# Chunk 1's rows let go by the first q, k weight piece, and a new order of all engines

## The chip, the cores and the metric

The kernel runs on one core of a Trainium2 chip. The core has engines with instruction queues of their own: PE (matmul, with its weight load shown as PEld), DVE (vector), ACT (scalar), POOL (GpSimd) and SP, which here only issues DMAs; 16 DMA engines move the data. The metric is the device time of one execution in microseconds (us). Of the kernel before there are three runs: 194.37, 195.01 and 195.72 us, median 195.01.

## What is computed

A pre-norm transformer layer on 2048 rows of 512 channels in bf16: attention with 32 heads of 16 channels over a dilated window of 8 keys, then a gated feed-forward of width 1376. Cut to what matters:

```python
def _A_ref(x, wqkv, wo):
    H = 32; Dh = D // H; W, dil = 8, 2
    q, k, v = (x @ wqkv).reshape(B, S, 3, H, Dh)          # split in three, heads first
    idx = arange(S)[:, None] - arange(W)[None, :] * dil    # keys at s, s-2, ... s-14
    kg, vg = k[idx], v[idx]                                # masked where idx < 0
    attn = softmax(einsum("bhsd,bhswd->bhsw", q, kg) * Dh ** -0.5)
    return einsum("bhsw,bhswd->bhsd", attn, vg) @ wo

def _B_ref(x, W_gate, W_up, W_down):
    gate, up = x @ W_gate, x @ W_up
    return ((gate * (gate > 0)) * up) @ W_down

h  = x + _A_ref(layernorm(x), A_wqkv, A_wo)
h2 = h + _B_ref(layernorm(h), B_W_gate, B_W_up, B_W_down)
```

## The kernel before

The rows are worked in four chunks of 512 (`tk` = 0 to 3), each of four row blocks of 128. A chunk goes through these stages; the names in quotes are the plan's own keys for its steps.

- First layer norm: statistics and their aggregation on DVE ("xst", line 467; "xag", line 470), the root on ACT ("xrl", "xre"), for chunks 1 and 3 a bias on DVE ("xnb", line 488), the normalization on DVE for chunks 0 and 2 ("xxn", line 502) and on ACT for chunks 1 and 3 (line 499), then the transposition, on PE ("xtp", line 531) with an eviction by ACT ("xte") or, for chunk 0's row block 1, by DVE ("xtv", line 545). Chunk 3's transposition is done by DMA.
- q, k and v: twelve groups of matmuls (line 572), eight for q and k and four for v, each evicted by ACT (line 580). In chunk 0 the first six q, k groups are cut in three pieces ("qka", "qkb", "qkc"), so that the first two row blocks and the first two weight pieces can be used early. A matmul with 512 columns is a whole group's quarter; the pieces have 256.
- Scores: products of q with shifted keys on DVE ("pr"; in chunk 0 half steps at line 637, elsewhere line 620), summed over channels on PE ("sc1" for the far four keys and "sc0" for the near four, line 628, each over all its products), the exponential on ACT, for chunk 0 a mask on DVE ("mk").
- The spread of the weights by DMA from SP (line 756), products with shifted values on DVE ("mu"), their sum, of which the first step is an accumulating DMA from POOL ("ta", line 831), the division (line 795 in chunk 0), and the output projection on PE ("wo", line 867).
- Second layer norm, gate and up matmuls (line 940), their evictions and product, the down projection (line 990) and the output.

PE takes work of several chunks in turn: while DVE is busy with chunk 0's attention, PE does the q, k and v groups of chunks 1 to 3.

**What sets the order.** The program is written as a plan of 751 steps, each with an engine, a duration, its dependencies and the buffers that it takes. `RANK` holds one number for each step, in the order in which the plan adds them. An engine's steps are issued strictly in the order of their numbers; the planner's own times, which come from its table of durations and due times, only decide which buffer of a pool each step gets. `XT` and `WT` (lines 377 and 378) are those due times of the first loads: the four row blocks of chunk 0, the four of chunk 1, chunks 2 and 3; and of the weights.

**The first loads.** They are issued by hand, ahead of the plan, in lines 316 to 347. SP and ACT each issue two of chunk 0's row blocks and two of the four pieces of the q, k weight, in turn: block 0 and piece 0 on SP, block 1 and piece 1 on ACT, block 2 and piece 2 on SP, block 3 and piece 3 on ACT. Everything behind these goes out on SP, held back by gates: POOL copies a few bytes into the place that a later load will fill, from a place that an earlier load fills. The later load must wait for that copy, and the copy for the earlier load.

```python
nc.gpsimd.tensor_copy(out=x_sm[0:1, BPC:2 * BPC, 0:1], in_=x_sm[0:1, 3, 0:BPC])      # line 334
for j in range(BPC, 2 * BPC):
    nc.sync.dma_start(x_sm[:, j:j + 1, :], x_rows[:, j:j + 1, :])                    # line 336
nc.gpsimd.tensor_copy(out=wv_sb[0:1, 0, 0:1], in_=wqk_sb[0:1, 3, 0:1])               # line 337
nc.sync.dma_start(wv_sb[:], w3_r[:, :, 2 * D:3 * D])
nc.gpsimd.tensor_copy(out=x_sm[0:1, 2 * BPC, 0:1], in_=x_sm[0:1, 2 * BPC - 1, 0:1])  # line 339
```

So chunk 1's four row blocks wait for chunk 0's block 3, the v weight for piece 3 of the q, k weight, and the rows of chunks 2 and 3 (and, on SP behind them, the output projection's weight and the gate weight) for chunk 1's last row block. Before chunk 0's first q, k matmul PE runs matmuls on a blank tile (lines 421 and 429).

Of the kernel before, what the change touches and what calls it, by code (L numbers as in the profile page):

```python
# [16 lines left out]

RANK = [
# [38 lines left out]
]  # L57


# [143 lines left out]
def kernel(  # L203
# [11 lines left out]
    nc = tc.nc  # L215
# [24 lines left out]
    BPC = CS // P  # L240
# [25 lines left out]
    x_sm = sb.tile([P, NTB, D], BF16, name="x_sm")  # L266
    wqk_sb = sb.tile([P, NT, 2 * D], BF16, name="wqk_sb")
# [45 lines left out]
    def setup():  # L313

        w3_r = A_wqkv.rearrange("(dt p) f -> p dt f", p=P)
        for i in range(2):
            for n, q in enumerate((nc.sync, nc.scalar)):
                j = 2 * i + n
                q.dma_start(x_sm[:, j:j + 1, :], x_rows[:, j:j + 1, :])
                q.dma_start(wqk_sb[:, j:j + 1, :], w3_r[:, j:j + 1, 0:2 * D])  # L320
        nc.scalar.preload_act_table_set("natural_log_exp_and_others")
        V.memset(warm[:], 0.0)
        make_identity(nc, identity[:])
        nc.gpsimd.memset(eps_t[:], EPS)
        nc.gpsimd.iota(ci[:], pattern=[[0, 1]], base=0, channel_multiplier=1)
        nc.gpsimd.iota(sel_i[:], pattern=[[1, H]], base=0, channel_multiplier=0)
        nc.gpsimd.iota(sp_i[:], pattern=[[1, H], [0, DQ]], base=0, channel_multiplier=0)
        nc.gpsimd.iota(sm_i, pattern=[[0, 4], [1, H]], base=0, channel_multiplier=0)
        nc.gpsimd.iota(mk_i[:], pattern=[[1, PADL]], base=0, channel_multiplier=0)
        nc.gpsimd.memset(kT[:, :, 0:PADL], 0.0)  # L330
        nc.gpsimd.memset(vT[:, :, 0:PADL], 0.0)


        nc.gpsimd.tensor_copy(out=x_sm[0:1, BPC:2 * BPC, 0:1], in_=x_sm[0:1, 3, 0:BPC])
        for j in range(BPC, 2 * BPC):
            nc.sync.dma_start(x_sm[:, j:j + 1, :], x_rows[:, j:j + 1, :])  # L336
        nc.gpsimd.tensor_copy(out=wv_sb[0:1, 0, 0:1], in_=wqk_sb[0:1, 3, 0:1])
        nc.sync.dma_start(wv_sb[:], w3_r[:, :, 2 * D:3 * D])
        nc.gpsimd.tensor_copy(out=x_sm[0:1, 2 * BPC, 0:1], in_=x_sm[0:1, 2 * BPC - 1, 0:1])
        for tk in range(2, NCK):  # L340
            nc.sync.dma_start(x_sm[:, tk * BPC:(tk + 1) * BPC, :], x_rows[:, tk * BPC:(tk + 1) * BPC, :])

        nc.sync.dma_start(wo_sb[:], A_wo.rearrange("(p t) f -> p t f", t=NT))
        for n in "gud":
            for i in range(2):
                if n not in LATE:
                    f_load(n, i)


        for n, (op, by) in enumerate(((ALU.arith_shift_right, 2), (ALU.bitwise_and, H - 1),  # L350
                                      (ALU.arith_shift_right, 5))):
            V.tensor_scalar(out=tmp[:, n:n + 1], in0=ci[:], scalar1=by, scalar2=None, op0=op)
        V.tensor_copy(out=cf[:, 0:3], in_=tmp[:])
        V.tensor_scalar(out=cf[:, 2:3], in0=cf[:, 2:3], scalar1=1.0 * DIL, scalar2=None, op0=ALU.mult)
        V.tensor_scalar(out=cf[:, 3:4], in0=cf[:, 2:3], scalar1=4.0 * DIL, scalar2=None, op0=ALU.add)
        V.tensor_scalar(out=sel[:], in0=sel_i[:], scalar1=cf[:, 0:1], scalar2=None, op0=ALU.is_equal)
        V.tensor_scalar(out=spread[:], in0=sp_i[:], scalar1=cf[:, 1:2], scalar2=None, op0=ALU.is_equal)
        V.tensor_scalar(out=same[:], in0=sm_i, scalar1=cf[:, 1:2], scalar2=None, op0=ALU.is_equal)
        for hf in range(2):
            V.tensor_scalar(out=mask[:, hf, :], in0=mk_i[:], scalar1=cf[:, 2 + hf:3 + hf],  # L360
                            scalar2=None, op0=ALU.is_ge)
# [12 lines left out]
    TDD, TDL = 1.3, 1.5  # L374
    NWARM, NFILL = 56, (13, 10, 0)
    NHALF = 6
    XT = (3.47, 3.64, 5.45, 5.97, 8.4, 8.7, 9.25, 9.75, 15.9, 17.65)
    WT = (7.65, 7.65, 5.0, 13.7, 19.0, 24.95, 22.4, 28.8)
    DMAT = (('h',2,0),('h',2,2),('h',3,0),('h',3,2),('h',1,0),('x',3,0),('x',3,2))

    EARLY = (1, 2, 3)
# [695 lines left out]
```

## Time and profile before

| | |
|---|---|
| median of three runs | 195.01 us (194.37 to 195.72) |
| the profiled execution | 196.09 us |
| its span, first to last instruction | 194.2 us |
| granted PE clock | 1.000 |
| DMA moved | 24.61 MB, mean 127 GB/s |
| HBM read, written | 8.42 MB, 2.10 MB |

The profile is of one execution. Times in it are microseconds from the span's start. "Busy" is the time an engine spent in instructions; matmuls are pipelined and their ends are modelled, so for PE the distance from start to start says more than a duration. A row names the source line, the engine, the operation, and the tile written and read. "Idle before, releaser" is how long an engine waited ahead of an instruction and what ended that wait. The chain of waits is followed back from the last instruction, at each step to what released it.

### The profile page before, as it was taken

The numbers are of one execution on the slowest core, as the hardware profiler recorded it, in microseconds if no ns is written. First come the engines' busy times: TensorE is split into PE (matmuls) and PEld (weight loads), VectorE is DVE, ScalarE is ACT, GpSimd is POOL, SyncE is SP. The second block draws the span as 40 slices with busy tenths as digits, with TensorE's granted clock in tenths as the row PEclk, the third lists the DMA queues.
The fourth block names the chain that finished last, engine by engine and source line by source line (L and its number), as shares of the span: only waits on it lengthen the run. The fifth ranks groups of instructions, "written<-read, shape, count | busy, mean of one in ns | idle before, by whom it ended". The sixth has DMA issues, their size and how long they took to land.

```text
span 194.2 us, 3099 instructions
## 1 busy us (share of the span) xinstructions
PE 188.5 (97%) x1141; PEld 98.3 (51%) x1141; DVE 150.7 (78%) x243; ACT 115.7 (60%) x241; POOL 17.0 (9%) x35
## 2 busy tenths in 40 slices
PE   7897999999999999999999999999999999999994
PEld 7884455555445344644454444445454444554443
DVE  6769999999999999979999988699966424021432
ACT  3568989964799682974362679612875911267500
POOL 3000001420000004200046000001100000000000
PEclk9999999999999999999999999999999999999999
DMA  5759776999900807996169935733400141203021
GB/s 194 205 164 358 262 168 127 181 192 246 378 29 16 199 4 147 190 181 161 27 122 187 202 64 153 173 81 57 108 0 0 34 101 57 81 0 108 0 64 47
DMA packets 25214, 24.61 MB, mean 127 GB/s; under 512 B 11408, under 2 KB 21488, under 8 KB 25200
## 3 DMA queue, kind: packets, MB, share of 16 engines
q1 hardware_dynamic: 22176, 16.26, 30.1%
q0 software_dynamic: 2304, 7.34, 20.6%
q10 hardware_dynamic: 720, 0.82, 1.3%
q8 instruction: 9, 0.15, 0.3%
q14 instruction: 5, 0.04, 0.1%
HBM read 8.42 MB, written 2.10 MB: 54 GB/s over the span
## 4 chain that ended last, share of the span: by engine, by line
PE 89%; DMA 5%; ACT 2%; issue 1%; DVE 1%; SPq 1%; ACTq 0%; POOL 0%
PE bank L940 36%; PE bank L990 20%; PE bank L572 17%; PE bank L867 7%; DMA x_sm<-in_A_x_dram 5%; PE bank L628 4%; PE bank L907 3%; PE bank L531 2%; ACT row L499 1%; DVE st L467 1%; SPq L336 1%; ACT quad L580 0%; PE bank L713 0%; PE bank L870 0%; ACT kT L580 0%
## 5 line engine op out<-in xcount | busy, mean ns | idle before, releaser
L940 PE MATMUL bank<-quad,wgu_sb 128*128 128x512 bf16 x320 | 72.4, 379 | 0.0
L940 PEld LDWEIGHTS <-wgu_sb 128*128 128x128 bf16 x320 | 31.0, 98 | 36.7 <-issue 1.3
L990 PE MATMUL bank<-wd_sb,gT 128*128 128x512 bf16 (+3 forms) x198 | 39.1, 355 | 0.0
L947 ACT ACTIVATE gr<-bank 128x512 bf16<-128x512 f32 x40 | 23.8, 607 | 22.6 <-PE bank L940 21.0
L572 PE MATMUL bank<-quad,wqk_sb 128*128 128x512 bf16 (+1 forms) x152 | 29.3, 345 | 0.3 <-ACT rs L480 0.3
L990 PEld LDWEIGHTS <-gT 128*128 128x128 bf16 (+1 forms) x198 | 18.5, 98 | 19.7
L944 ACT CAST up_sb<-bank 128x512 bf16<-128x512 f32 x40 | 22.7, 597 | 8.7 <-PE bank L940 5.3
L788 DVE TENSOR_TENSOR big<-big,vT 128x4096 bf16<-128x4096 bf16 x12 | 27.0, 2285 | 0.7 <-DVE big L620 0.5
L620 DVE TENSOR_TENSOR big<-quad,kT 128x4096 bf16<-128x4096 bf16 x12 | 27.1, 2286 | 0.0
L968 DVE TENSOR_TENSOR gT<-gr,up_sb 128x1024 bf16<-128x1024 bf16 x20 | 13.7, 689 | 16.4 <-ACT up_sb L944 13.4
L572 PEld LDWEIGHTS <-wqk_sb 128*128 128x128 bf16 x152 | 16.8, 113 | 10.9 <-issue 0.5
L831 POOL DMA_DIRECT2D big<-big x12 | 10.9, 1016 | 76.1 <-DVE row L728 29.4
L791 DVE TENSOR_TENSOR big<-big 128x1024 bf16<-128x1024 bf16 (+2 forms) x24 | 16.9, 729 | 0.3 <-DMA big<-big 0.3
L572 PE MATMUL bank<-quad,wv_sb 128*128 128x512 bf16 x64 | 15.7, 380 | 0.0
L867 PE MATMUL bank<-wo_sb,quad 128*128 128x512 bf16 x64 | 15.4, 379 | 0.0
L1003 DVE TENSOR_TENSOR row<-x_sm,bank 128x512 bf16<-128x512 bf16 (+2 forms) x10 | 5.5, 579 | 10.7 <-PE bank L990 10.7
L580 ACT CAST quad<-bank 128x512 bf16<-128x512 f32 x16 | 9.5, 609 | 5.6 <-PE bank L572 5.6
L467 DVE BATCH_NORM_STATS2 st<-x_sm 128x6 f32<-128x512 bf16 x16 | 10.4, 680 | 2.9 <-DMA x_sm<-in_A_x_dram 2.9
L456 ACT ACTIVATE row<-x_sm,mv 128x512 bf16<-128x512 bf16 x12 | 8.6, 716 | 6.1 <-DVE mv L448 5.8
L547 ACT COPY quad<-bank 128x1024 bf16<-128x1024 bf16 (+1 forms) x10 | 8.8, 910 | 4.9 <-PE bank L531 4.9
L878 DVE SCALAR_TENSOR_TENSOR x_sm<-x_sm,bank 128x512 bf16<-128x512 bf16 x12 | 8.2, 686 | 3.9 <-PE bank L867 3.6
L502 DVE TENSOR_SCALAR row<-x_sm,mv,rs 128x512 bf16<-128x512 bf16 x24 | 8.6, 407 | 2.3 <-ACT rs L484 2.3
(78 smaller groups left out, 171.0 us busy)
## 6 DMA issues: line engine op xcount, KB each, us to landing
big<-big POOLq DMA_DIRECT2D x12, 512.0 KB, 5.9
big<-ex SPq DMA_DIRECT2D x32, 128.0 KB, 2.8
wgu_sb<-in_B_W_gate_dram SPq DMA_DIRECT2D x2, 688.0 KB, 7.8
wgu_sb<-in_B_W_up_dram SPq DMA_DIRECT2D x2, 688.0 KB, 8.6
wd_sb<-in_B_W_down_dram SPq DMA_DIRECT2D x2, 640.0 KB, 5.8
x_sm<-in_A_x_dram SPq DMA_DIRECT2D x2, 512.0 KB, 4.0
x_sm<-up_sb POOLq DMA_DIRECT2D x4, 256.0 KB, 3.7
out_dram<-x_sm SPq DMA_DIRECT2D x4, 256.0 KB, 2.2
```

The source lines that it names most:

```text
L467: V.bn_stats(out=st.t[:], in_=x_sm[:, tk * BPC + j, :])
L572: nc.tensor.matmul(mm.t[:, lo:hi], lhsT=wv_sb[:, dt, t:D:NT] if c == 2 else wqk_sb[:, dt, c * D + t:(c + 1) * D:NT], rhs=xnT.t[:, dt, lo:h ...
L620: V.tensor_tensor(out=pb.t[:].rearrange("p (t w) s -> p t w s", t=2), in0=q4, in1=k4, op=ALU.mult)
L788: V.tensor_tensor(out=mt.t[:], in0=ab.t[:], in1=v8, op=ALU.mult)
L791: V.tensor_tensor(out=mt.t[:, 0:n, :], in0=mt.t[:, 0:n, :], in1=mt.t[:, n:2 * n, :], op=ALU.add)
L831: nc.gpsimd.dma_start(mt.t[:, 0:4, :], mt.t[:, 4:8, :], accum_op=ALU.add)
L867: nc.tensor.matmul(od.t[:], lhsT=OT.t[:, t, j * P:(j + 1) * P], rhs=wo_sb[:, t, :], start=(t == 0), stop=(t == NT - 1 and tk not in RPE))
L940: nc.tensor.matmul(mm.t[:fs, lo:hi], lhsT=wgu_sb[:, dt, g, ft * P: ft * P + fs], rhs=hnT.t[:, dt, lo:hi], start=(dt == 0), stop=(dt == NT ...
L944: nc.scalar.copy(out=ub.t[:fs, i, :], in_=um.t[:fs, :])
L947: nc.scalar.activation(out=gr.t[:fs, i, :], in_=gm.t[:fs, :], func=ACT.Relu)
L968: V.tensor_tensor(out=gt.t[:fs, 0:n, :], in0=gr.t[:fs, 0:n, :], in1=ub.t[:fs, 0:n, :], op=ALU.mult)
L990: nc.tensor.matmul(od.t[:, c0:c1], lhsT=gts[ft].t[:fs, ft % 2, j * P:(j + 1) * P], rhs=wd_sb[:fs, ft, c0:c1], start=(ft == 0), stop=(ft == ...
```

## The change

Three things in the text of the kernel. The gate of chunk 1's rows (line 334) copies from piece 0 of the q, k weight instead of chunk 0's block 3. The due times `XT` and `WT` have new values for chunk 1's blocks, for chunks 2 and 3, and for five of the weights. And `RANK` has new numbers, for nearly all steps from the 35th on; every engine's order changes. No step is added or taken away.

```diff
 RANK = [
     0, 1, 2, 3, 4, 5, 6, 7, 8, 9, 10, 11, 12, 13, 14, 15, 16, 17, 18, 19,
-    20, 22, 23, 25, 29, 31, 32, 21, 24, 26, 28, 30, 36, 39, 40, 27, 33, 35, 37, 42,
-    47, 51, 34, 38, 41, 43, 46, 50, 55, 44, 54, 59, 63, 45, 57, 61, 65, 48, 67, 70,
-    74, 52, 56, 64, 71, 80, 83, 88, 90, 81, 86, 89, 93, 76, 82, 73, 79, 95, 116, 92,
...
+    20, 22, 23, 25, 29, 31, 32, 21, 24, 26, 28, 30, 36, 39, 42, 27, 33, 35, 37, 40,
+    44, 47, 34, 38, 41, 43, 45, 50, 54, 48, 56, 58, 61, 46, 51, 59, 66, 63, 73, 75,
+    77, 55, 62, 68, 79, 53, 71, 80, 89, 90, 91, 93, 96, 76, 81, 82, 87, 109, 118, 98,
...
-        nc.gpsimd.tensor_copy(out=x_sm[0:1, BPC:2 * BPC, 0:1], in_=x_sm[0:1, 3, 0:BPC])
+        nc.gpsimd.tensor_copy(out=x_sm[0:1, BPC:2 * BPC, 0:1], in_=wqk_sb[0:1, 0, 0:BPC])
         for j in range(BPC, 2 * BPC):
             nc.sync.dma_start(x_sm[:, j:j + 1, :], x_rows[:, j:j + 1, :])
...
-    XT = (3.47, 3.64, 5.45, 5.97, 8.4, 8.7, 9.25, 9.75, 15.9, 17.65)
-    WT = (7.65, 7.65, 5.0, 13.7, 19.0, 24.95, 22.4, 28.8)
+    XT = (3.47, 3.64, 5.45, 5.97, 7.8, 8.2, 8.65, 9.1, 14.8, 16.5)
+    WT = (7.75, 7.75, 5.0, 12.5, 18.0, 24.95, 21.4, 28.8)
```

Sorted for each engine, the start of the two orders reads as follows (the number behind the point is the chunk; what stands in brackets is the row block, counted from 0 through all chunks, or which of q, k, v and which head group, t = 0 to 3):

```
PE before: transposes of block 0, blanks, block 1, blanks, qka (q0, k0), block 2, qka (q1), block 3, qka (k1), qkb (q0, k1, k0), qkc (q0, k0, k1), ...,
           two whole q, k groups, the rest of q2, k2, v1, v0, block 6, sc1.0, blocks 7, 4, 5, v3, v2, sc0.0, ...
PE after:  transposes of block 0, blanks, block 1, blanks, block 2, qka (k0, q0), block 3, qkb (k0), qka (q2, k1), qkb (q0), qkc (q0, k0), ...,
           v3 between the rest of the q, k groups, v2, v1, blocks 6, 5, 7, sc1.0, block 4, v0, sc0.0, ...
DVE before: ..., xtv (block 1), xxn (blocks 2, 3), xst (blocks 4, 5, 7, 6), pr1, pr1, xnb.1, pr0, pr1, pr1, pr0, pr0, mk1, pr0, ...
DVE after:  ..., xxn (block 2), xtv (block 1), xxn (block 3), xst (blocks 6, 5, 4, 7), pr0, pr1, xnb.1, pr1, pr0, pr1, pr1, pr0, pr0, mk1, ...
```

68 rows, old and new, of the table RANK are left out of this document.

## The prediction

> **What bounds the kernel now.** I read the page first, then a table of stretches, then the chain of waits from its start.
>
> ```profile
> span 194.2 us, 3099 instructions
> ...
> PE 188.5 (97%) x1141; PEld 98.3 (51%) x1141; DVE 150.7 (78%) x243; ACT 115.7 (60%) x241; POOL 17.0 (9%) x35
> ```
>
> The table has one row for each stretch: its length, then busy time and instruction count of PE, its weight load, DVE, ACT and POOL, then clock, DMA share and GB/s.
>
> ```profile
> 24.00:84.00 60.00, 60.00 (x368) 30.12 (x367) 58.64 (x77) 46.81 (x97) 7.58 (x10) 1.00 0.69 158
> 24.00:191.43 167.43, 167.41 (x926) 81.97 (x924) 130.85 (x198) 99.95 (x211) 14.57 (x18) 1.00 0.50 112
> ```
>
> From 24 us to 191.43 us PE idles 0.02 us, at clock 1.00. An order can win nothing there; it can only lose. Whatever is to be won lies ahead of 24 us. DVE, 58.64 of 60 us busy from 24 to 84, runs almost as tight, so an order that shifts PE forward must shift DVE forward too. The chain of waits (start, length, what) says what the head waits for:
>
> ```profile
> 1.66 5.15 DMA x_sm<-in_A_x_dram
> 6.82 0.05 issue
> 6.87 0.20 POOL x_sm L334
> ...
> 8.41 4.03 DMA x_sm<-in_A_x_dram
> 12.44 0.02 issue
> 12.46 1.29 DVE st L467 x2
> ```
>
> Chunk 0's fourth row block lands at 6.82, POOL's gate lets chunk 1's rows go, the last of them is issued at 8.41 and lands at 12.44; then come its statistics. The chain goes on through ACT's normalization to PE's first transpose of chunk 1, which is the row at 18.98 of PE's own time order (start, busy, step and count; in brackets the idle time before):
>
> ```profile
> 8.27 0.60 PE L572 MATMUL bank<-quad,wqk_sb 128*128 128x256 bf16 x4 [0.33 <-ACT rs L480]
> ...
> 9.37 6.49 PE L572 MATMUL bank<-quad,wqk_sb 128*128 128x256 bf16 x50
> 15.69 1.89 PE L572 MATMUL bank<-quad,wv_sb 128*128 128x512 bf16 x8
> 18.98 0.40 PE L531 MATMUL bank<-identity,row 128*128 128x128 bf16 x4 [1.40 <-ACT row L499]
> ...
> 22.86 1.05 PE L628 MATMUL bank<-big,sel 128*32 128x512 bf16 x16
> ```
>
> The 50 matmuls from 9.37 to 15.69 are 42 of 256 columns and 8 of 512, so one of 512 takes 6.32 / 29 = 0.22. The eight from 15.69 would be through at 15.69 + 8 x 0.216 = 17.42, and the next step starts at 18.98: **the stall is 1.56 from start to start**. It is the only one of size on PE after 8.27, and the whole prize.
>
> **The change, part by part.**
>
> *The gate.* Landings, from the rows of two source lines (durations of the issue, first and last issue; then time to landing): SP's two q, k pieces, and chunk 1's four row blocks.
>
> ```profile
> L320 SPq DMA_DIRECT2D wqk_sb<-in_A_wqkv_dram x2: 416/424/432, 1.2 to 2.1; - x2
> ...
> DMA to landing us min/median/max: 3.4/4.4/5.3
> ```
>
> ```profile
> L336 SPq DMA_DIRECT2D x_sm<-in_A_x_dram x4: 328/430/431, 7.1 to 8.4; - x4
> ...
> DMA to landing us min/median/max: 2.1/2.5/4.0
> ```
>
> The first q, k piece lands at 1.2 + 3.4 = 4.6 (the shorter time is the first one's: both stand in one queue), and the gate's copy takes 0.20 as before, so SP issues the four row blocks at about 4.86, 5.29, 5.72 and 6.15 (0.43 apart) instead of 7.1 to 8.4: 2.2 us earlier. They need not land 2.2 earlier: SP's other piece, issued at 2.1, is under way until 2.1 + 5.3 = 7.4. By the shortest and longest landing of these same rows, the third block lands between 7.8 and 9.7 and the fourth between 8.2 and 10.2. I take 8.5 and 9.0, just behind the 7.4.
>
> *DVE.* Its time order:
>
> ```profile
> 7.73 0.39 DVE L545 COPY quad<-bank 128x512 bf16<-128x512 bf16 x1
> 8.04 0.79 DVE L502 TENSOR_SCALAR row<-x_sm,mv,rs 128x512 bf16<-128x512 bf16 x2
> ...
> 12.46 1.29 DVE L467 BATCH_NORM_STATS2 st<-x_sm 128x6 f32<-128x512 bf16 x2 [1.71 <-DMA x_sm<-in_A_x_dram]
> ...
> 13.95 2.33 DVE L637 TENSOR_TENSOR big<-quad,kT 128x2048 bf16<-128x2048 bf16 x2
> ...
> 48.51 0.75 DVE L795 TENSOR_TENSOR quad<-big,rec 128x512 bf16<-128x512 bf16 x2
> ...
> 61.10 1.38 DVE L502 TENSOR_SCALAR row<-x_sm,mv,rs 128x512 bf16<-128x512 bf16 x4
> ```
>
> The two rank lists, sorted for each engine, give DVE's new order. It keeps the four statistics of chunk 1 ahead of the first product of q and k, but takes the third row first (blocks 6, 5, 4, 7). DVE is free for them at 8.04 + 0.79 = 8.8. Statistics and aggregations of two blocks take 13.95 - 12.46 = 1.5 today, with a third block's aggregation in it, so four end near 11.7. The third block's late bound, 9.7, would make that 12.6; the fourth block is only needed at 8.8 + 1.9 = 10.7. The products also need the evicted first q and k:
>
> ```profile
> 11.37 1.08 ACT L580 CAST kT<-bank 128x512 bf16<-128x512 f32 x2
> ```
>
> The first key row's eviction is the first of these two and ends at 11.9 (they are half of 1.08 apart); PE comes to that work no later than now, since chunk 0's fourth block, whose transposes it needs, keeps its time. So the products start near 11.95 instead of 13.95, **DVE gains 2.0** (1.35 at the late bound); its wait of 1.71 goes.
>
> *PE's start.* The list swaps the copy of row block 1 (7.73 today) with the normalization of block 2, half of the 0.79: the copy ends 0.31 to 0.39 later, I take 0.31 because the copy itself is followed after 8.04 - 7.73 = 0.31, and the first q, k matmul goes from 8.27 to 8.58. Block 2's transposes, four matmuls of 128 columns or 0.22 by the rate above, stand behind four such matmuls today and now fill part of that wait. **Loss 0.09.**
>
> *PE's stall.* Up to the score matmuls of the first half (22.86 today) both orders hold the same steps: 22.86 - 8.27 - 1.56 = 13.03 us of work. New: 8.58 + 13.03 - 0.22 = 21.39, if nothing waits. What could wait: three of the four v steps now stand ahead of chunk 1's first transpose, which moves it to about 18.7. It needs ACT's normalization of the third block; ACT's first one follows DVE's bias step, which stands two products behind the start, 11.95 + 2.33 = 14.3, and with two evictions (0.54 each) and two normalizations it ends near 17. Covered by 1.6; without that cover PE would wait the difference. The other scores need six products: 11.95 + 6 x 1.15 + 0.1 = 18.95, and PE arrives one score step (0.98, 22.86 to the next step), one v step and one row block's transposes before the 21.39, at 19.3. The first half's need eight, 11.95 + 9.3 = 21.25 against 21.39; at the late bound 21.9, a wait of 0.5. So 22.86 becomes 21.4 to 21.9: **PE gains 1.47, at least 0.95.**
>
> *v and the later loads.* The gate of v, on POOL, keeps its condition, the fourth q, k piece:
>
> ```profile
> 7.67 0.18 POOL L337 COPY wv_sb<-wqk_sb 1x1 bf16<-1x1 bf16 x1 [0.61 <-DMA wqk_sb<-in_A_wqkv_dram]
> ```
>
> But SP is no longer busy with rows until 8.8, so v goes out about 1 us earlier. Its first use in the new order is at 8.58 + 6.3 = 14.9 (the like of 58 matmuls of 256 columns at 0.109), today 15.69. Nothing, and v may be a microsecond late. The loads of chunks 2 and 3 wait for chunk 1's last row, so they go out near 9.2 instead of after 12.44; their first statistics stand behind all eight products on DVE. Nothing.
>
> *The rest of the order.* 198 of PE's 233 planned steps change place, 149 of DVE's 219, 25 of SP's 43, 8 of POOL's 17. PE's total is the same, so the question is only whether its dense part stays dense. I compared the tight meetings of DVE and PE. The first output projection comes at 50.02 today, DVE's last product for it ends at 48.51 + 0.75 = 49.26. In the new list it stands one q, k step (0.86) earlier on PE: 50.02 - 1.47 - 0.86 = 47.7, against 49.26 - 2.0 = 47.26. Slack 0.4 where it is 0.76 now. The second layer norm's transposes:
>
> ```profile
> 61.69 1.24 PE L531 MATMUL bank<-identity,row 128*128 128x128 bf16 x16
> ```
>
> They keep their place in PE's work, 60.2; DVE's four normalizations before them begin 0.34 earlier in its work, 61.10 - 0.34 - 2.0 = 58.8, so the slack grows. On POOL the accumulating DMAs of chunk 0 run in another order (second tile first), on SP the second up-weight load passes a down-weight load and chunk 3's spread passes chunk 0's output: each with its user microseconds behind. Nothing. The tail after PE's last step is the same set of small pieces. Nothing.
>
> **Sum:** 0 elsewhere, -1.47 at the head: span 194.2 to 192.7. The profiled execution took 196.09, 1.9 more than its span, so 194.6 on that footing. The median of the runs is 195.01, and they spread from 194.37 to 195.72, 1.35, close to the stall's size. The last row took 4.0 to land, the median of the four 2.5; had it taken that, it would have landed at 10.9, the products would have started near 12.3, and PE's stall would nearly vanish. So I read the stall as present in the longest of the three runs and mostly absent in the shortest. 195.72 - 1.47 = 194.25 and 194.37 less a few tenths (the 0.3 by which 12.3 is late of 11.95) agree; if every run has it, 195.01 - 1.47 = 193.5. I take **194.0**, own range 193.4 to 194.6.
>
> *A rule against it.* From the table of stretches:
>
> ```profile
> 5.00:6.00 1.00, 1.00 (x22) 1.00 (x20) 0.50 (x3) 0.50 (x2) 0.00 (x0) 1.00 0.95 284
> ```
>
> The DMA engines are 0.95 busy (and move 284 GB/s) in a microsecond into which the rows move. The Trainium skill (Trainium Kernel Development and Optimization, Key Constraints) says that DMAs from SP, ACT and POOL share the same 16 engines and interleave. By that rule the early rows take turns with block 3 of chunk 0 on ACT's queue; it is the third rival, and the sum gets its 1.7; by the landings it gets nothing. For the landings: SP's own second q, k piece is under way until 7.4 in any case, so ACT's queue has the same rival up to 6.82 with or without the rows. The skill's DMA: Bandwidth & Descriptors (Queues, rings and completion order) has each engine go round the queues that have work; no run here shows it yet.
>
> **The rivals.**
> *The dense part leaks.* PE waits at the first output projection or later, because DVE's lead is less than 2.0. At the late bound it is 1.35: the scores then wait 0.5 and the projection, put back as much, nothing or a few tenths; two or three such waits make 0.5 to 1.0, so 194.5 to 195.0. For it: 0.02 us of idle time is hard to repeat, DVE's 98%. Against: almost every meeting keeps its place.
> *The rows land no earlier.* The gate opens, but the rows stand behind the weights and land like today. Then the products start at 13.95 as now, and the first half's scores come at 13.95 + 9.3 = 23.25, 0.4 behind today's 22.86, since the new list has all eight ahead of the mask step: 195.01 + 0.4 = 195.4. For it, the 0.95; against, 7.4 is the end of SP's weights and 12.44 is far behind it.
> *Early rows starve chunk 0.* Slower than before. 512 KB at 284 GB/s are 1.8 us; if all of it goes ahead of block 3, that lands at 8.6 instead of 6.82 and its statistics start 1.7 later, with the copy that releases PE queued behind them on DVE. PE starts near 10.3: 194.0 + 1.7 = 195.7. It decides from a landing of 6.9 on; every 0.1 beyond costs 0.1, and past 7.9 the gain is gone.
> *Full size everywhere.* The median run has all of the stall and the 0.33 of idle time ahead of 8.27 goes too, with a tenth of the small steps between: 195.01 - 1.56 - 0.33 - 0.1 = 193.0.
>
> **How the numbers follow.** Forecast 0.58; leak 0.18; no earlier 0.08; starved 0.08; full size 0.08. About 1%, 1.95 us, is what a measurement can tell from no change: under 193.06 is faster, over 196.96 slower. Faster: the full-size case and the forecast's low edge, 0.09. Slower: starvation with the largest leak ends at 196.7, beside the line, 0.05. Same: 0.86. The range 193.1 to 195.4 leaves out the starved and the full-size case.
>
> **What would show it.** Right: rows issued from 4.9 and landed by 10; first q, k matmul at 8.5 to 8.7; first product of q and k at 11.9 to 12.5; no PE idle time over 0.4 between 9 and 24 us; score matmuls of the first half at 21.4 to 21.8; the first output projection at 47.7. Wrong: chunk 0's block 3 landing after 6.9, a new bracket on PE behind 24 us, or the last matmul less than 1 us earlier than today.

## The result, and the profile after

| | before | after |
|---|---|---|
| median of 20 runs each | 194.81 us (194.37 to 197.61) | 196.04 us (194.86 to 199.97) |
| ratio, 95% interval | | 1.0041 [1.0023, 1.0060] |
| the profiled execution | 196.09 us | 195.56 us |
| its span | 194.2 us | 193.4 us |

The ratio leaves out one slow run on each side (197.61 and 199.97) and is not the quotient of the medians, which would be 1.0063. By it the changed kernel is slower by 0.4%, or 0.8 us, where the prediction had it faster by half a per cent. The two profiled executions say the opposite of the medians: before's was among its longer ones, after's among its shorter ones. A difference of two single profiles is therefore no measure of this change; what the profiles can show is which waits there are.

The page of after, first part, and the rows of the table of stretches that answer to before's (columns as there):

```profile
span 193.4 us, 3099 instructions
...
PE 188.8 (98%) x1141; PEld 98.4 (51%) x1141; DVE 150.0 (78%) x243; ACT 115.7 (60%) x241; POOL 21.7 (11%) x35
```

```profile
24.00:84.00 60.00, 59.82 (x366) 29.82 (x364) 57.72 (x73) 46.28 (x96) 12.28 (x10) 1.00 0.69 158
24.00:190.60 166.60, 166.42 (x921) 81.31 (x918) 128.67 (x193) 98.88 (x208) 19.28 (x18) 1.00 0.50 111
```

The dense part is no longer dense: 0.18 us of idle time shows on PE, all of it between 24 and 84 us (ends of matmuls are modelled, so from start to start it is more, below), and DVE has lost 0.92 us of busy time there (58.64 before). POOL is the only engine that got busier: 12.28 instead of 7.58. The chain of waits after 33 us shows the same from its own side; in before it runs through PE there:

```profile
33.36 6.17 DMA big<-big
...
42.46 5.08 POOL wgu_sb L849
47.73 4.50 DVE big L620 x2
52.26 0.59 ACT kT L580
52.88 0.63 DVE big L620
```

A copy of four elements on POOL holds DVE, and an eviction on ACT stands between two products of DVE. The head is as forecast. The rows' line and PE's time order:

```profile
L336 SPq DMA_DIRECT2D x_sm<-in_A_x_dram x4: 327/430/441, 5.2 to 6.5; - x4
...
DMA to landing us min/median/max: 2.5/2.7/2.9
```

```profile
8.86 0.60 PE L572 MATMUL bank<-quad,wqk_sb 128*128 128x256 bf16 x4
...
18.64 0.83 PE L531 MATMUL bank<-identity,row 128*128 128x128 bf16 x12
19.40 1.05 PE L628 MATMUL bank<-big,sel 128*32 128x512 bf16 x16
...
21.57 1.05 PE L628 MATMUL bank<-big,sel 128*32 128x512 bf16 x16
...
47.86 1.03 PE L867 MATMUL bank<-wo_sb,quad 128*128 128x512 bf16 x4
...
57.94 0.38 PE L713 MATMUL bank<-row,same 128*128 128x512 bf16 x1 [0.18 <-DVE row L728]
```

The stall ahead of 18.98 is gone, the first half's scores come at 21.57 and the projection at 47.86. The bracket at 57.94 is new. DVE's and POOL's time order in the stretch behind it:

```profile
12.14 2.36 DVE L637 TENSOR_TENSOR big<-quad,kT 128x2048 bf16<-128x2048 bf16 x2 [0.39 <-ACT kT L580]
...
44.85 1.96 DVE L791 TENSOR_TENSOR big<-big 128x1024 bf16<-128x1024 bf16 x4
46.73 0.75 DVE L795 TENSOR_TENSOR quad<-big,rec 128x512 bf16<-128x512 bf16 x2
47.73 4.50 DVE L620 TENSOR_TENSOR big<-quad,kT 128x4096 bf16<-128x4096 bf16 x2 [0.25 <-POOL wd_sb L850]
52.14 0.15 DVE L448 TENSOR_SCALAR mv<-sm 128x1 f32<-128x1 f32 x1
52.88 2.29 DVE L620 TENSOR_TENSOR big<-quad,kT 128x4096 bf16<-128x4096 bf16 x1 [0.59 <-ACT kT L580]
```

```profile
42.46 5.08 POOL L849 COPY wgu_sb<-big 1x4 bf16<-1x4 bf16 x1 [3.32 <-DVE big L791]
47.47 0.22 POOL L850 COPY wd_sb<-big 1x11 bf16<-1x11 bf16 x1
```

Lines 849 and 850 are gates of the same kind as line 334: they copy a few elements out of a buffer of chunk 0's attention into the places of the later up and down weights. The same copy took 0.20 us before:

```profile
42.77 0.20 POOL L849 COPY wgu_sb<-big 1x4 bf16<-1x4 bf16 x1 [1.80 <-DVE big L791]
```

DVE's product at 47.73 needs that buffer, so it waits for both copies. The eviction that DVE waits for at 52.88 writes chunk 3's k for t = 2, and itself waited 0.27 for DVE's product before (ACT's order):

```profile
52.26 0.59 ACT L580 CAST kT<-bank 128x512 bf16<-128x512 f32 x1 [0.27 <-DVE big L620]
```

One number separates the head from the rest in every profile of this study. Up to the first half's scores both orders hold the same PE work, so **the span less the start of those score matmuls** is the time of everything behind them, free of when the first rows came. The table holds it for all profiles; the start is the row of line 628 that is told as "first half" above, the span that of the page.

| kernel | first half's scores | span | behind them |
|---|---|---|---|
| before, before again | 22.86, 21.83 | 194.2, 193.3 | 171.3, 171.5 |
| after, after again | 21.57, 21.51 | 193.4, 193.8 | 171.8, 172.3 |
| early gate alone, twice | 21.92, 20.84 | 193.1, 192.0 | 171.2, 171.2 |
| early gate and due times | 22.56 | 194.5 | 171.9 |
| new order with the late gate | 22.50 | 194.9 | 172.4 |
| new order in the head only; behind it only | 21.41; 21.57 | 193.1; 194.0 | 171.7; 172.4 |
| after, k eviction early; copies on ACT | 21.95; 21.58 | 193.6; 193.0 | 171.7; 171.4 |
| after, both repairs | 22.64 | 194.4 | 171.8 |
| old head, new order behind it, both repairs | 22.04 | 193.2 | 171.2 |

171.2 is the dense value; the changed order adds 0.6 and 1.1 to it. The 171.9 of the early gate with the due times comes from a wait that is told with that run.

### The profile page after: what moved, and what is told of

Its sections match the earlier page's. It is cut to its first block, busy times and chain, and to the rows that moved or that the text cites. A ratio compares the mean times of both kernels' runs of the same rounds, so it can differ in the third digit from the quotient of the medians.

```text
span 193.4 us, 3099 instructions
## 1 busy us (share of the span) xinstructions
PE 188.8 (98%) x1141; PEld 98.4 (51%) x1141; DVE 150.0 (78%) x243; ACT 115.7 (60%) x241; POOL 21.7 (11%) x35
## 4 chain that ended last, share of the span: by engine, by line
PE 81%; DMA 6%; DVE 5%; issue 3%; POOL 3%; SPq 0%; ACT 0%; POOLq 0%
PE bank L940 36%; PE bank L990 20%; PE bank L572 13%; PE bank L867 5%; DVE big L620 4%; DMA big<-big 3%; PE bank L628 3%; PE bank L907 3%; POOL wgu_sb L849 3%; DMA x_sm<-in_A_x_dram 2%; PE bank L531 2%; PE bank L713 1%; DVE row L502 0%; DVE st L467 0%; ACT kT L580 0%
## 5 line engine op out<-in xcount | busy, mean ns | idle before, releaser
L940 PE MATMUL bank<-quad,wgu_sb 128*128 128x512 bf16 x320 | 71.5, 379 | 0.0
L572 PE MATMUL bank<-quad,wqk_sb 128*128 128x512 bf16 (+1 forms) x152 | 29.9, 346 | 0.0
L580 ACT CAST kT<-bank 128x512 bf16<-128x512 f32 x16 | 9.5, 593 | 2.0 <-DVE big L620 1.5
```

Source lines behind the costliest of these rows:

```text
L572: nc.tensor.matmul(mm.t[:, lo:hi], lhsT=wv_sb[:, dt, t:D:NT] if c == 2 else wqk_sb[:, dt, c * D + t:(c + 1) * D:NT], rhs=xnT.t[:, dt, lo:h ...
L580: nc.scalar.copy(out=o, in_=mm.t[:])
L940: nc.tensor.matmul(mm.t[:fs, lo:hi], lhsT=wgu_sb[:, dt, g, ft * P: ft * P + fs], rhs=hnT.t[:, dt, lo:hi], start=(dt == 0), stop=(dt == NT ...
```

## The experiments

Ratios are to runs of before on the same chip in the same series.

**Controls.** Before and after once more, unchanged.

> The kernel before, unchanged, for a second profile and a control. Theory 1 (the stall at 17.4 was there only because chunk 1's last row landed at 12.44, and in most executions it lands near 10.9): time 194.4 to 195.0, span 192.5 to 193.1 if the profile falls on a typical execution, last row landed before 11.2, the first product of q and k at 12.0 to 12.6 and no idle time of PE over 0.5 between 9 and 24 us. Theory 2 (the stall is in every execution, and the new kernel loses elsewhere): products again at 13.5 or later and PE idle 1 us or more near 18.

> The changed kernel, unchanged, for a second profile. Its first profile (span 193.4) is shorter than its median run would have (196.04 less 2.1, 193.9). Both theories: about 196.0, ratio 1.003 to 1.007. If the loss is in the dense part, PE shows 0.5 to 1.5 us of idle time behind 24 us, with POOL's copy at line 849 taking several us as in the first profile (5.08); if it is in the head, the score matmuls of the first half start later than 21.9.

Before: 195.73 against 195.38 us, 1.0008 [0.9971, 1.0046]. After: 196.39, 1.0048 [1.0013, 1.0082]; the slowdown repeats. The new profile of before is the more telling one (line 336, then PE's time order):

```profile
L336 SPq DMA_DIRECT2D x_sm<-in_A_x_dram x4: 327/430/432, 6.7 to 8.0; - x4
...
DMA to landing us min/median/max: 2.1/2.3/2.6
```

```profile
16.30 1.89 PE L572 MATMUL bank<-quad,wv_sb 128*128 128x512 bf16 x8
18.03 0.39 PE L531 MATMUL bank<-identity,row 128*128 128x128 bf16 x4
18.35 1.05 PE L628 MATMUL bank<-big,sel 128*32 128x512 bf16 x16
```

The rows land within 2.6 us here, not 4.0, and PE has no stall at all ahead of chunk 1's transpose (16.30 + 8 x 0.216 = 18.03). The stall that was to be the whole prize is not in this execution of the unchanged kernel. That is Theory 1's picture; its ranges for the time (up to 195.0) and the span (up to 193.1) were missed by 0.7 and 0.2 us.

**The early gate alone.** Before, with one line of the change:

```diff
-        nc.gpsimd.tensor_copy(out=x_sm[0:1, BPC:2 * BPC, 0:1], in_=x_sm[0:1, 3, 0:BPC])
+        nc.gpsimd.tensor_copy(out=x_sm[0:1, BPC:2 * BPC, 0:1], in_=wqk_sb[0:1, 0, 0:BPC])
```

> The kernel before with only line 334 changed: the old order, the early rows. Theory 1 (early rows are good, the order loses): 194.0 to 194.6, ratio 0.994 to 1.000, less scatter than before, rows landed by 9.2. Theory 2 (early rows take the DMA engines from chunk 0's blocks 2 and 3 and its q, k pieces): 195.5 to 196.2, ratio 1.003 to 1.007, with block 3 or the q, k pieces landing 0.5 us or more later than before.

194.84 us against 195.38, 0.9981 [0.9951, 1.0011]. Once more, in another series:

> Before with line 334's source changed, as in the earlier run, now with five rounds. Theory (typical executions have the stall near 18 us only in part, so the gate alone is worth 0.2 to 0.5 us): a ratio of 0.997 to 0.999, with the interval under 1. Rival (it was the draw of that run): 0.9995 to 1.001.

194.62 against 194.89, 0.9971 [0.9942, 1.0000]. The first interval includes 1 and the second ends at it; their mean, 0.9976, with the half widths of 0.0030 and 0.0029 taken as independent, is uncertain by 0.0021. So the gate alone gains about 0.45 us, with anything from 0.1 to 0.9 open. The stretch from 24 to 84 us of the second run (columns as above) has no idle time on PE:

```profile
24.00:84.00 60.00, 60.00 (x369) 30.07 (x368) 58.53 (x71) 47.51 (x99) 7.60 (x10) 1.00 0.69 156
```

**The new order with the late gate.** After, with line 334 as before:

```diff
-        nc.gpsimd.tensor_copy(out=x_sm[0:1, BPC:2 * BPC, 0:1], in_=wqk_sb[0:1, 0, 0:BPC])
+        nc.gpsimd.tensor_copy(out=x_sm[0:1, BPC:2 * BPC, 0:1], in_=x_sm[0:1, 3, 0:BPC])
```

> The changed kernel with line 334 as before: the new order, the late rows. Theory 1 (the order loses, and early rows were its cover): 196.2 to 197.2, ratio 1.007 to 1.013, first product at 12.9 or later, since block 6 is taken first and ACT has the root of chunk 1 ahead of two evictions. Theory 2 (early rows lose): 194.4 to 195.2, ratio 0.997 to 1.002.

196.56, 1.0059 [1.0025, 1.0093]. Gate and order pull in opposite directions, and the order is the larger; the ratio lies below Theory 1's range, which began at 1.007. Its profile adds a wait that after's does not show, for chunk 3's rows, which SP transposes by DMA:

```profile
35.90 1.89 PE L572 MATMUL bank<-quad,wqk_sb 128*128 128x512 bf16 x8 [0.76 <-DMA quad<-row]
```

**The two halves of the order.** Both have the early gate and the new due times. The first takes the new order of PE, DVE and ACT up to the first half's scores, their mask step and the last eviction of chunk 0's v, and before's order behind them; SP and POOL as before. The second is its mirror, with SP and POOL as after.

```diff
 RANK: PE up to "sc0", DVE up to "mk0", ACT up to chunk 0's last eviction
-  after's numbers everywhere
+  first:  after's order up to there, before's order behind, SP and POOL before's
+  second: before's order up to there, after's order behind, SP and POOL after's
```

> Early rows; PE, DVE and ACT in the new order up to the near score matmuls of chunk 0, their mask and v's last eviction, and in the old order from there on; SP and POOL in the old order. Theory A (the new order loses behind 25 us): 194.3 to 194.9, ratio 0.994 to 1.000, like the early gate alone, PE without an idle time over 0.3 behind 24 us. Theory B (the new order loses in the head): 195.7 to 196.5, ratio 1.003 to 1.008.

> The mirror image: early rows; the old order up to that point, the new one from there on, SP and POOL in the new order. Theory A: 195.9 to 196.6, ratio 1.004 to 1.009, with PE waiting 0.3 or more at the denominators of chunk 1 (line 713 near 57.5) and POOL's copy at line 849 taking about 5 us. Theory B: 194.3 to 195.0, ratio 0.995 to 1.000.

New head: 196.04 against 195.05, 1.0045 [1.0014, 1.0075]. New tail: 196.38, 1.0063 [1.0039, 1.0087]. Each half costs. But the two losses don't add up to that of the whole: against the early gate alone (0.9976) they are 0.7% and 0.9%, and after's is 0.7%. So a half order can have waits that after does not have. Of what was expected of the new tail neither came, the copy of about 5 us (it took 2.20) nor PE's wait at line 713. The waits of PE behind 24 us, in its time order, first the new head:

```profile
34.43 1.89 PE L572 MATMUL bank<-quad,wqk_sb 128*128 128x512 bf16 x8 [0.38 <-DMA quad<-row]
```

and the new tail:

```profile
54.65 1.05 PE L628 MATMUL bank<-big,sel 128*32 128x512 bf16 x16 [0.47 <-ACT kT L580]
55.91 1.02 PE L572 MATMUL bank<-quad,wv_sb 128*128 128x512 bf16 x3 [0.21 <-ACT row L456]
```

In the new tail DVE does not wait for POOL's copies. There the eviction of chunk 3's k (t = 2) waits for DVE's first product of chunk 2, which in after comes behind it (ACT's order):

```profile
54.01 0.58 ACT L580 CAST kT<-bank 128x512 bf16<-128x512 f32 x1 [2.03 <-DVE big L620]
```

PE's 0.47 is for this eviction. For the head's wait the slack of one chain is the first thing to see. SP's spreads of chunk 0's first weights stand ahead of chunk 3's transposes on its queue, and start when the first mask step is through. The start of that chain with the early gate and before's order, and with the new head (start, duration, step, count):

```profile
20.91 6.08 SPq L756 DMA_DIRECT2D big<-ex  x8
```

```profile
21.33 5.61 SPq L756 DMA_DIRECT2D big<-ex  x8
27.04 3.94 SPq L520 DMA_TRANSPOSE quad<-row  x3
```

With before's head the chain starts 21.92 - 20.91 = 1.01 us ahead of the first half's scores, with the new one 21.41 - 21.33 = 0.08. It is the same in all profiles of the study with the early gate: 1.0 with the old head, 0.1 with the new. The new head puts the mask step behind all eight products instead of seven, and the SP queue loses 0.9 us of slack towards PE, which comes to chunk 3's groups as early as ever.

The lost slack alone does not make the bracket. PE goes on 0.13 or 0.14 us after the last of the four transposes lands. That transpose takes 2.4 or 2.5 us from issue to landing in nine of the fourteen profiles, 2.7 in one, and 3.2 or 3.3 in four; these four are the ones with a bracket at chunk 3's rows (the new order with the late gate, the new head, and two that follow: after with both repairs, and the early gate with the due times). In the four, and in the one with 2.7, the first packets of POOL's accumulating DMA (line 831) start 1.97 to 2.00 us after the transpose is issued; in the nine, 2.15 us or later. With a transpose of 2.4, the new head leaves PE a wait of about 0.2 at most, as in the second profile of after. So the head's wait is that of two transfers which meet, and the 0.9 us made the meeting likelier. This is read from the traces; no run moved that DMA.

**The mutual waits of DVE and ACT.** After, with ACT's eviction of chunk 3's k (t = 2) directly behind the one before it:

```diff
-    210, 200, 260, 212, 266, 193, 237, 273, 312, 233, 253, 197, 206, 279, 328, 318, 311, 330, 340, 470,
+    210, 200, 210.5, 212, 266, 193, 237, 273, 312, 233, 253, 197, 206, 279, 328, 318, 311, 330, 340, 470,
```

> The changed kernel with one number changed: ACT evicts chunk 3's third key group (k, t = 2) some ten steps earlier, near 40 instead of at 52.3, where it stood between two products of DVE (one ended at 52.2, the next started at 52.9, 0.59 late). Theory A: DVE runs its products through without that wait, PE's wait at line 713 (0.35 and 0.47 in the two profiles) and most of the 0.17 at the next transposes go, 0.3 to 0.6 less than the changed kernel: ratio to the kernel before 1.000 to 1.004. Rival (that wait has slack behind it and costs nothing): as the changed kernel, 1.004 to 1.007, with PE's wait at 713 still there.

195.89 against 195.05, 1.0026 [0.9995, 1.0057]. DVE's wait at 52.88 and PE's at 57.94 are gone (DVE's order of this kernel):

```profile
48.58 4.49 DVE L620 TENSOR_TENSOR big<-quad,kT 128x4096 bf16<-128x4096 bf16 x2 [0.24 <-POOL wd_sb L850]
52.99 0.15 DVE L448 TENSOR_SCALAR mv<-sm 128x1 f32<-128x1 f32 x1
53.06 2.28 DVE L620 TENSOR_TENSOR big<-quad,kT 128x4096 bf16<-128x4096 bf16 x1
```

**POOL's long copy.** After, with the two gates on ACT:

```diff
-                nc.gpsimd.tensor_copy(out=wgu_sb[0:1, :, 1, 0:1], in_=mt.t[0:1, 0:1, 0:NT].rearrange("p a s -> p s a"))
-                nc.gpsimd.tensor_copy(out=wd_sb[0:1, :, 0:1], in_=mt.t[0:1, 0:1, 0:NFT].rearrange("p a s -> p s a"))
+                nc.scalar.copy(out=wgu_sb[0:1, :, 1, 0:1], in_=mt.t[0:1, 0:1, 0:NT].rearrange("p a s -> p s a"))
+                nc.scalar.copy(out=wd_sb[0:1, :, 0:1], in_=mt.t[0:1, 0:1, 0:NFT].rearrange("p a s -> p s a"))
...
-            lg = add(("lg", tk), "POOL", 0.3, f_lg, [oev[NT - 1]], apr, use=[mt], lat=0.1)
+            lg = add(("lg", tk), "ACT", 0.3, f_lg, [oev[NT - 1]], apr, use=[mt], lat=0.1)
```

> The changed kernel with the two small copies that let the down and up weights go (lines 849 and 850) on ACT instead of POOL. Theory A (POOL's copy cannot run while DVE works without a pause): the copies take under 0.5 each instead of 5.08, the weights go out 2 to 4 us earlier than at 47.7, DVE's product at 47.73 starts 0.25 earlier, 0 to 0.25 less than the changed kernel: ratio 1.003 to 1.006. Rival (the late weights and not DVE's wait are what costs): 0.5 or more less, 0.998 to 1.002.

195.61 against 195.05, 1.0033 [1.0006, 1.0061]. On ACT the copy takes 0.20 us, and DVE's product no longer waits for it:

```profile
45.50 0.20 ACT L849 COPY wgu_sb<-big 1x4 bf16<-1x4 bf16 x1
```

By the intervals neither repair alone is told from after. Nor do the profiles price the two waits one by one: with the copies on ACT, PE's wait at line 713 is gone too, although DVE still waits for the eviction, longer than before:

```profile
52.50 2.29 DVE L620 TENSOR_TENSOR big<-quad,kT 128x4096 bf16<-128x4096 bf16 x1 [0.71 <-ACT kT L580]
```

From the score matmuls near 53 us (line 628, the first that start behind 50) to the span's end it is 140.3 us in after, 139.9 with the copies on ACT, 139.7 with the k eviction early and 139.6 with the early gate alone. Either repair alone leaves little of the loss there.

**Both repairs, and both with before's head.** The second is the mirror kernel above (before's order up to the first half's scores, the new order behind) with the same two edits.

> The changed kernel with both repairs at once: the two small copies of lines 849 and 850 on ACT, and the eviction of chunk 3's k (t = 2) on ACT directly behind the one before it. Theory (POOL's long copy and the mutual waits of DVE and ACT are the tail's loss, and the rest is the new head's 0.3 to 0.5 at chunk 3's transposed rows): no wait of DVE for POOL or ACT between 47 and 54 us, no wait of PE at lines 713 and 502, a ratio to before of 0.999 to 1.001, that is 0.4% under the changed kernel. Rival 1 (each repair frees only what the other gives back, as their single runs of 1.0026 and 1.0033 suggest): 1.0025 to 1.0035. Rival 2 (the order costs in the head alone): 1.0025 or more, with the tail dense in the profile.

> Early rows, the old order of PE, DVE and ACT up to the first half's scores, the new order behind, with both repairs. Theory (head and tail of the new order each cost, and both are now repaired): no wait of PE for chunk 3's transposed rows near 34 us and none for ACT near 54 us; a ratio to before of 0.996 to 0.999, beside the early gate alone (0.998). Rival (the seam of old head and new tail is itself what cost in the mirror run, 1.0063): 1.003 or more.

After with both: 195.34 against 194.89, 1.0010 [0.9981, 1.0039]. With before's head too: 194.82, 0.9975 [0.9949, 1.0001]. Both ratios are where the theories had them. The first interval still holds Rival 1's 1.0025 to 1.0035, and the step from the first kernel to the second, 0.35%, is within their intervals. With the new head one wait of PE is left from 24 us on, that for the transposed rows:

```profile
35.79 1.89 PE L572 MATMUL bank<-quad,wqk_sb 128*128 128x512 bf16 x8 [0.51 <-DMA quad<-row]
```

With the old head there is none (stretch from 24 to 84 us):

```profile
24.00:84.00 60.00, 60.00 (x369) 30.18 (x368) 58.50 (x76) 47.13 (x99) 7.05 (x8) 1.00 0.68 157
```

The mirror kernel went from 1.0063 to 0.9975 by the two repairs, some 1.7 us, with intervals well apart. Since DVE did not wait for POOL's copy in the mirror kernel's profile, the eviction is the likely part of it. The rival, that the seam of two orders was itself the cost, falls with it.

**The due times.** The early gate alone, with the new due times besides; they can only change which buffer of a pool a step gets:

```diff
-    XT = (3.47, 3.64, 5.45, 5.97, 8.4, 8.7, 9.25, 9.75, 15.9, 17.65)
-    WT = (7.65, 7.65, 5.0, 13.7, 19.0, 24.95, 22.4, 28.8)
+    XT = (3.47, 3.64, 5.45, 5.97, 7.8, 8.2, 8.65, 9.1, 14.8, 16.5)
+    WT = (7.75, 7.75, 5.0, 12.5, 18.0, 24.95, 21.4, 28.8)
```

> Before with line 334's source and the due times XT and WT changed, with the old ranks: only buffers of the pools can come out differently. Theory (the due times are harmless, the ranks carry the loss): the same ratio as line 334 alone, 0.997 to 0.999. Rival (the other buffers bring waits, and make part of what the two half orders lost): 1.002 or more.

194.86 against 194.89, 0.9992 [0.9964, 1.0020]: between the two expectations, not decided. At most a small part of the loss is theirs, since the repaired kernel with the old head has them too and is at 0.9975. But the profile, of the longest of this kernel's twelve executions (196.45), has the wait for chunk 3's rows, and it has before's head and the full 1.0 us of slack:

```profile
35.80 1.89 PE L572 MATMUL bank<-quad,wqk_sb 128*128 128x512 bf16 x8 [0.60 <-DMA quad<-row]
```

SP's spreads took 6.73 us here and not 6.08, so the transposes came 0.65 late, and the last met POOL's accumulating DMA and took 3.3. So the new head is not the only way into this wait, and before's head is no sure way out of it.

## Why the prediction was wrong

**The gate, DVE and PE's start: right.** The rows were issued 5.2 to 6.5 us and were in within 2.9 us of issue; chunk 0's third block was in at 6.17 and its fourth (block 3) at 5.98, so nothing was starved in this execution. The first product came at 12.14 (forecast 11.95), the first half's scores at 21.57 (21.39), the projection at 47.86 (47.7). The first q, k matmul came at 8.86 rather than 8.58, since the rows of that execution were later than in before's. The cost of the swap can be read against the landing of chunk 0's third block: 8.86 - 6.17 = 2.69 with the new head; with the early gate alone that block landed at 6.60 and the matmul came at 8.97, 2.37. The 0.32 agrees with the 0.31 of the sum, and what is left of it at the first half's scores, 21.57 - 6.17 = 15.40 against 21.92 - 6.60 = 15.32, with its 0.09. The chain of waits of after, then of the early gate alone, has these landings (start of the transfer, length):

```profile
1.69 4.48 DMA x_sm<-in_A_x_dram
```

```profile
1.68 4.92 DMA x_sm<-in_A_x_dram
```

**The prize: mis-sized.** The sum took 1.0 us off the median, for a stall of 1.56 "present in the longest of the three runs and mostly absent in the shortest". The gate alone is worth 0.45 us in the median, and the second profile of before has no stall. The spread of the runs has another source: without the stall the gate's two profiles still stand 193.1 and 192.0 apart, all of it ahead of the first half's scores (21.92 and 20.84), and the profiles have chunk 0's third block land up to 7.24 us (early gate with the due times). Whether the early rows have a part in that is open: with the late gate this block landed at 5.5 to 6.1 us in three profiles, with the early one at 5.4 to 7.2 in eleven, and the fourth (block 3) behind 6.9, the sign of the rival *Early rows starve chunk 0*, in two of the eleven (7.05 and 7.47). The new order of the head gains nothing on top: it comes 0.09 later to the same scores. What the gate does remove is a chance: with the late gate chunk 1's last row landed at 12.44, 10.51 and 12.65 us in the three profiles (the last is of the new order, where PE then waited 0.79 for chunk 1), with the early gate at 9.88 or before in all eleven.

**The rest of the order: the step that failed.** The prediction compared two meetings of DVE and PE, found slack, and put everything else at "Nothing". Meetings of three other pairs suffered:
- *POOL with DVE.* "On POOL the accumulating DMAs of chunk 0 run in another order" is all that was said. The gates of lines 849 and 850 were taken as free, because they had been in before. In the new order they fall into a stretch where DVE runs without a pause, the copy takes 5.08 us, and DVE's next product waits for it, 0.25.
- *ACT with DVE.* The eviction of chunk 3's k (t = 2) moved to between DVE's last product of chunk 1 and its first of chunk 2. In `kT` it shares no element with either: those products, of t = 2 and 3, read one chunk's columns of both, the eviction writes chunk 3's of t = 2, which lie between them in memory. They wait for each other all the same, in whichever order they stand (in after the eviction 0.27 and the next product 0.59, in the mirror kernel the eviction 2.03); that the wait is set by the range from first to last address is my reading of the product's form and was not tried. With the eviction early both waits are gone.
- *SP with PE, and with POOL.* "Chunk 3's spread passes chunk 0's output: each with its user microseconds behind" looked at what passes what on SP, not at when its chain starts. It starts 0.9 later towards PE. Chunk 3's transposed rows then miss PE by 0.38 and 0.51 in the two kernels shown above, where the last of them met POOL's accumulating DMA; in after's own two profiles they miss it by nothing and by 0.2.

Taken together: from the gate alone (0.9971 and 0.9981) to after (1.0041 and 1.0048) are 0.7%, 1.35 us. Both repairs give back 0.3% to 0.4%, the old head a further 0.35%; each of these steps is about as large as its uncertainty. Clear of it are the mirror kernel's 0.9% by the two repairs, and the new head's 0.7% against the gate alone (0.5% against the early gate with the due times, which it has too). Of that second one the profile, of the shortest of the twelve executions, shows 0.5 us, and where the rest goes stays open.

The rival "The dense part leaks" was the right one, with 0.18 where it should have led, and its mechanism was wrong: not DVE's lead over PE was too short, three other pairs were. Its price of 0.5 to 1.0 us is near what the profiles show behind the first half's scores (0.6 and 1.1); what made its time too low was that it set this price against a prize of 1.0 to 1.5. With the prize measured, 0.45, it would have read 194.81 - 0.45 + 0.6 to 1.0, or 195.0 to 195.4, still under the 196.04 (and under the 195.6 that the ratio gives). That median is longer than the profiled execution by 0.5; what such a run waits for besides was not traced. The new bracket on PE behind 24 us, which was named as a sign of error, is there.

**The version that beats both** is the smallest: before, with line 334 alone, at 194.62 and 194.84 us (by the ratio 0.9976, uncertain by 0.0021). The repaired order with the old head is level with it (0.9975), so the new order has won nothing beyond the gate.

## What to carry to other kernels

An order found by a planner, in a kernel whose bounding engine has 0.02 us of idle time in 167, can only keep that or lose it; take the one edit that removes a wait, and leave the order alone unless it has to follow. When many steps move, don't only check the tightest pair of engines: list each step that crosses a neighbour it shares a buffer or a tile with, on POOL and SP too, with its slack in before's trace, and each pair of transfers that the new times bring together. And ask of the stall that is to be removed whether a second execution shows it, before it is counted.

## What was not expected of the hardware

A POOL copy of four elements took 5.08 us in both profiles of after, with the k eviction early and with the late gate, and 0.19 or 0.20 where DVE had a pause of 0.1 us (42.71 to 42.81 in before). It began 0.15 us into a DVE product, and ended when DVE next paused, at 47.48, seven DVE instructions later. In the kernel with the new tail only it took 2.20, to the end of the one product it had begun under:

```profile
42.30 2.20 POOL L849 COPY wgu_sb<-big 1x4 bf16<-1x4 bf16 x1 [3.34 <-DVE big L791]
```

The Trainium skill (SBUF — State Buffer, Who interferes with whom) says that a DVE instruction with two SBUF inputs contends with a GpSimd instruction that reads SBUF. For the two-port modes of DVE it also says that whoever issues first has the shared ports for the whole instruction. The 2.20 looks like such a block of one whole instruction; the 5.08 goes beyond it, since the block outlasted one instruction and held through seven that followed each other without a gap. All of those have two SBUF inputs. Why the copy got in after one product in the new tail is open: DVE's eight instructions there are the same, started at the same distances.

In both profiles where a row of chunk 1 took 4.0 or 4.2 us, 15 of the 16 parts of that load had landed by 10.77 us and the last came 1.7 or 1.9 later, and a transfer of 16 KB on the queue for instructions began while the load was under way (10.22 and 9.66 us). In the other twelve profiles it began when the last row was in, or later. No run moved it, so that it held the row up is not shown.

The four row blocks of chunk 1 can land far apart though they are issued evenly: in before's profile the longest took 4.0 us and the median 2.5, in the second profile 2.6 and 2.3. That one difference made and removed the stall on which the prediction was built.
